# A new table of order and engine choices for an RWKV attention and Fourier-mixing kernel

## The chip, the cores and the metric

The kernel runs on one core of a Trainium2 chip. The metric is the device time of one execution in microseconds (us). A core has five engines with queues of their own, each in program order: TensorE (PE; its weight loads are listed as PEld), VectorE (DVE), ScalarE (ACT), GpSimd (POOL) and SyncE (SP), which here only issues transfers. ScalarE and GpSimd issue some transfers too. Semaphores order the engines among each other.

## The reference

Four batches, eight heads, 768 time steps, head size 48. First a linear attention with decay, then over its output x a two-dimensional Fourier transform of which the real part is added, a normalisation, and a two-layer network (384 to 1536 to 384) with a residual:

```python
for t in range(S):
    cur = np.einsum('bhd,bhe->bhde', u[None] * kt, vt)
    y[:, :, t] = np.einsum('bhd,bhde->bhe', rt, state + cur)
    state = w[None, :, :, None] * state + np.einsum('bhd,bhe->bhde', kt, vt)
...
X = np.fft.fft(np.fft.fft(x, axis=1), axis=2)
u = x + np.real(X)
un = (u - mu) / np.sqrt(var + 1e-06)
return u + np.maximum(un @ w_ch1, 0.0) @ w_ch2
```

## The kernel before

The time steps are cut into 24 chunks of 128 (six to a batch). For each chunk i: k, r and v are loaded (on SP). VectorE multiplies k and r by tables of decay powers into the bf16 tile KR (line 373, both operands in SBUF; the first two chunks in two halves, line 364, partly on GpSimd). KR is transposed to KRT, by TensorE and a copy (lines 393 to 398) for chunks 0 to 11, by a transposing DMA on SP (line 384) for 12 to 23. VectorE makes PR, the product of the k half and the r half of KRT (line 409, both operands in SBUF). TensorE makes the scores A (line 419) into two PSUM banks, one for the even heads and one for the odd ones; each is masked into MA either by a copy AC on ScalarE (line 426) and a select on GpSimd (line 428), or by VectorE straight out of PSUM (line 431). A bonus term de (line 482) is copied to DE (ScalarE, line 492) and multiplied with V into TT (GpSimd, line 493). The masked scores times V and the carried state make y (line 504). X is y plus TT: on VectorE as an addition (line 512), or, with TT added by an identity matmul `xt` (line 507) on TensorE, as a copy on ScalarE (line 514). The state S is carried on from chunk to chunk.

When the chunks of a batch are there, VectorE folds X into HH and XF (lines 527 and 533 for batch 0, chunk by chunk; 551, 558 and 566 for the others: all with both operands in SBUF). TensorE does the transform over time (fp, line 598), the result is evacuated to TT2 (ScalarE, line 606, or VectorE, line 607), reversed into TR (617), and TensorE transforms over the model dimension (mp, line 637). UF is x plus the result (VectorE, line 649, or ScalarE, line 652, behind an identity matmul `xr`), UB a bf16 version (lines 656 to 661), `st` and `MV` the statistics (666, 668). UB is transposed to UNT, by TensorE and a copy (676 to 680) for batch 0, by DMA for the others. A half batch (384 steps) is one unit hf of the network: 12 groups hp of three matmuls (line 713) with a Relu into HT on ScalarE (718) or VectorE (719), then for three row blocks j four groups mo of three matmuls each (line 733), the evacuation osb on VectorE (line 740) and the store (line 744 from GpSimd, 745 from SP).

Each of these steps is an entry in a list of operations with a number and, for some, several alternatives of engine. The table ORDER (line 97 on) gives the sequence in which the entries are emitted: `1123` is operation 1123 with its first alternative, `1124.1` the same with the second. `emit` plays it in that order: it hands each new tile the buffer of its ring that comes free first in the table, so the table decides the order in each engine's queue, the engine, and the buffers and PSUM banks. The operations numbered 0 to 149 are dummy matmuls over zeros (line 259, `idle`), of which a table takes as many as it likes.

```python
for k, (n, a) in enumerate(order):
    o = self.ops[n]
    for t in o["new"]:
        ends = held[t.ring]
        m = min(range(len(ends)), key=ends.__getitem__)
        ends[m] = last[t]
        t.value = self.rings[t.ring][m] if t.view is None else t.view(self.rings[t.ring][m])
    fn = o["alts"][a][2]
    if fn is not None:
        fn()
```

Of the kernel before, what the change touches and what calls it, by code (L numbers as in the profile page):

```python
# [97 lines left out]
170 152 158 173 159 160 166 193 162 150 163 161 171 168.1 174 151 175 153 0 1 2 182 205 155 164 165 154 183 186 187  # L98
172 202 203 178 185 167.1 169 156 184 199 200 299 3 4 5 6 7 8 302 303 300.1 190 9 304 305.1 188 10 307 191 189 192 196
274.1 275.1 310 195 206 208 209 325 11 12 329 327 328 330.1 331 13 14 15 332 198 214 333 16 339 179 340 277 350 279 17  # L100
18 352 278.1 280 282 201 276.1 207 326 335.1 287 157 353 311 281 334 197 289 336.1 285 181.1 211 212 354 375 223 355
308.1 290 21 22 283 356 286 19 20 377 180 291 204 379 378.1 380 23 24 25 382 381 288.1 309.1 385.1 306 215 400 292 284
194 26 27 293 301 312 213 220 294 295 314 376.1 28 402 315 313.1 342 317 210 337 383 341 343 403 404 405 224 338 357
358 316 386.1 29 407 464 364 365 389 408.1 409.1 217 218 351.2 362 318.1 319 320.1 344 296 345 410 177 468 366 226 384
390 363 391 466 467.1 367 469 30 31 471 392 406 412 387 360 423 33 388.1 32 425 426 427 221 443 216 361 445 446 347
447 413 401.1 368 176 297 346 359 369 298 411 35 428 34 430 370 448 450 431 348 433 227 485 321 322 323 393.1 394 371
372 395.1 219 424.2 487 415 324 414 374 416.1 488 271 396 273.1 417 418.1 489 373 397 37 490 419 36 813 806 807 349
222 1057 434 474 472 435 436.1 429 399 475 1055 814 815 799 800 816 792 437 438 229 230 451.1 452.1 420 422 232 421
398 449 491 506 432 801 233 802 444 453 793 794 795 796 797 817 818 798 819 803 804 808 809 810 470 527 439 440 805
# [693 lines left out]
```

## Time and profile before

| | |
|---|---|
| device time, median of 3 runs | 190.88 us (189.22 to 191.32) |
| the profiled execution | 190.09 us, of which its span is 188.2 us |
| mean granted TensorE clock | 0.989 of full speed |
| busy in the span: PE | 163.6 us (87%), 1592 matmuls |
| DVE | 150.1 us (80%), 350 instructions |
| ACT | 98.7 us (52%), 239 instructions |
| POOL | 84.2 us (45%), 124 instructions |

The span reaches from the first to the last instruction that the profile shows. A busy time is the time in which an engine ran at least one instruction. "Idle before" in a row is how long the engine stood still ahead of those instructions, with what released it. The granted clock is given as a share of full speed, 2.4 GHz.

### The profile page before, as it was taken

The numbers are of one execution on the slowest core, as the hardware profiler recorded it, in microseconds if no ns is written. First come the engines' busy times: TensorE is split into PE (matmuls) and PEld (weight loads), VectorE is DVE, ScalarE is ACT, GpSimd is POOL, SyncE is SP. The second block draws the span as 40 slices with busy tenths as digits, with TensorE's granted clock in tenths as the row PEclk, the third lists the DMA queues.
The fourth block names the chain that finished last, engine by engine and source line by source line (L and its number), as shares of the span: only waits on it lengthen the run. The fifth ranks groups of instructions, "written<-read, shape, count | busy, mean of one in ns | idle before, by whom it ended". The sixth has DMA issues, their size and how long they took to land.

```text
span 188.2 us, 4286 instructions
## 1 busy us (share of the span) xinstructions
PE 163.6 (87%) x1592; PEld 110.9 (59%) x1595; DVE 150.1 (80%) x350; ACT 98.7 (52%) x239; POOL 84.2 (45%) x124
## 2 busy tenths in 40 slices
PE   7987785947894996889899999899999999999990
PEld 1444463736772774566576677666677667666650
DVE  3479999997699999989989979998795868474240
ACT  3887566835872896654376765643384312311300
POOL 6748378491592453244761236576303411002131
PEclk9999999987999999999999999999999999999999
DMA  6999998999982996899999989891100361003222
GB/s 122 207 218 206 181 207 224 179 250 213 184 149 45 191 178 119 142 178 177 227 230 213 180 176 212 207 210 55 45 0 0 88 166 42 0 3 135 74 84 84
DMA packets 98341, 27.30 MB, mean 145 GB/s; under 512 B 95281, under 2 KB 96818, under 8 KB 98322
## 3 DMA queue, kind: packets, MB, share of 16 engines
q1 hardware_dynamic: 95808, 21.15, 58.1%
q0 software_dynamic: 2512, 5.90, 12.8%
q8 instruction: 12, 0.20, 0.4%
q14 instruction: 7, 0.06, 0.1%
q10 hardware_dynamic: 2, 0.00, 0.0%
HBM read 19.77 MB, written 4.72 MB: 130 GB/s over the span
## 4 chain that ended last, share of the span: by engine, by line
PE 44%; DVE 24%; issue 12%; DMA 10%; ACT 5%; POOL 2%; POOLq 0%; DVEq 0%; ACTq 0%
PE bank L713 17%; PE bank L733 12%; DMA KRT<-KR 8%; PE bank L598 4%; DVE PR L409 3%; DVE KR L373 3%; DVE X L512 2%; PE bank L637 2%; PE bank L259 2%; DMA UNT<-UB 2%; DVE MA L431 2%; POOL out_dram L744 2%; ACT AC L426 1%; PE bank L419 1%; DVE XF L533 1%
## 5 line engine op out<-in xcount | busy, mean ns | idle before, releaser
L713 PE MATMUL bank<-UNT,W 128*128 128x384 bf16 x288 | 54.2, 327 | 3.3 <-DVE X L512 2.4
L733 PE MATMUL bank<-W,HT 128*128 128x384 bf16 x288 | 52.7, 326 | 0.0
L718 ACT ACTIVATE HT<-bank 128x384 bf16<-128x384 f32 x67 | 30.1, 493 | 26.9 <-PE bank L713 25.6
L713 PEld LDWEIGHTS <-W 128*128 128x128 bf16 x288 | 30.8, 114 | 15.2 <-issue 3.5
L428 POOL TENSOR_SCALAR_AFFINE_SELECT MA<-AC 128x512 bf16<-128x512 bf16 x39 | 30.2, 780 | 17.7 <-ACT AC L426 17.4
L733 PEld LDWEIGHTS <-HT 128*128 128x128 bf16 x288 | 27.2, 98 | 16.4
L493 POOL TENSOR_TENSOR TT<-V,DE 128x384 bf16<-128x384 bf16 x24 | 21.6, 900 | 21.8 <-ACT DE L492 15.6
L426 ACT CAST AC<-bank 128x512 bf16<-128x512 f32 x39 | 22.3, 594 | 7.3 <-PE bank L419 5.8
L373 DVE TENSOR_TENSOR KR<-kr,wtab 128x768 bf16<-128x768 f32 x22 | 25.0, 1142 | 1.0 <-DMA kr<-in_r_dram 0.9
L744 POOL DMA_DIRECT2D out_dram<-osb x18 | 10.1, 561 | 33.6 <-DVE osb L740 31.4
L740 DVE SCALAR_TENSOR_TENSOR osb<-bank,rstd,UF 128x384 f32<-128x384 f32 x24 | 14.6, 611 | 11.2 <-PE bank L733 11.0
L719 DVE TENSOR_SCALAR HT<-bank 128x384 bf16<-128x384 f32 x29 | 15.2, 548 | 2.5 <-PE bank L713 2.5
L598 PE MATMUL bank<-te_t,XF 128*128 128x193 bf16 x108 | 13.7, 258 | 3.9 <-DVE XF L533 2.5
L259 PE MATMUL bank<-zero 128*128 128x512 bf16 x35 | 13.1, 468 | 2.7 <-DVE wuc L282 1.4
L409 DVE TENSOR_TENSOR PR<-KRT 128x512 bf16<-128x512 bf16 x24 | 14.5, 612 | 1.1 <-DMA KRT<-KR 0.5
L598 PEld LDWEIGHTS <-XF 128*128 128x128 bf16 x120 | 11.2, 105 | 6.1 <-DVE XF L533 2.7
L649 DVE SCALAR_TENSOR_TENSOR UF<-bank,X 128x384 f32<-128x384 f32 x22 | 11.5, 550 | 2.6 <-PE bank L637 2.4
L462 ACT CAST S<-bank 64x192 bf16<-64x192 f32 x30 | 9.4, 313 | 7.3 <-PE bank L450 4.0
L666 DVE BATCH_NORM_STATS2 st<-UF 128x6 f32<-128x384 f32 x24 | 13.0, 545 | 0.0
L419 PE MATMUL bank<-KRT 64*128 64x128 bf16 x192 | 9.8, 225 | 3.5 <-DMA KRT<-KR 2.3
L512 DVE TENSOR_TENSOR X<-bank,TT 128x384 bf16<-128x384 f32 x21 | 11.5, 546 | 1.6 <-PE bank L504 0.9
L419 PEld LDWEIGHTS <-KRT 64*128 64x128 bf16 x192 | 5.9, 97 | 11.2 <-issue 4.7
(95 smaller groups left out, 231.8 us busy)
## 6 DMA issues: line engine op xcount, KB each, us to landing
kr<-in_k_dram SPq DMA_DIRECT2D x24, 192.0 KB, 3.8
kr<-in_r_dram SPq DMA_DIRECT2D x24, 192.0 KB, 4.3
vt<-in_v_dram SPq DMA_DIRECT2D x24, 192.0 KB, 4.4
out_dram<-osb POOLq DMA_DIRECT2D x18, 192.0 KB, 2.3
W<-in_moe_w_ch_dram POOLq DMA_DIRECT2D x3, 384.0 KB, 5.0
W<-in_moe_w_ch_dram POOLq DMA_DIRECT2D x2, 576.0 KB, 7.5
out_dram<-osb SPq DMA_DIRECT2D x6, 192.0 KB, 1.9
te_t<-te_c SPq DMA_DIRECT2D x1, 579.0 KB, 5.4
```

The costliest lines, as they stand in the source:

```text
L259: op("idle", [("PE", "idle", lambda: nc.tensor.matmul(z(), lhsT=zero[:, 0:128], rhs=zero, start=True, stop=True))], r=["zero"], new=[z])
L373: one(("KR", i), "DVE", "KR", lambda: nc.vector.tensor_tensor(out=KR().rearrange("t s p (a d) -> t (s p) a d", a=2)[:, :, :, 0:D], in0=kr( ...
L409: one(("PR", i), "DVE", "PR", lambda: nc.vector.tensor_tensor(out=PR(), in0=KRT()[:, 0], in1=QTall(), op=AluOp.mult), r=kts, new=[PR], use ...
L419: nc.tensor.matmul(A_ps[a]()[:, p, :], lhsT=KRT()[rows, 0, p, :], rhs=QT(p, rows), start=(p == 0), stop=(p == NP - 1), skip_group_check=True)
L426: op(("AC", i, a), [("ACT", "AC", lambda: nc.scalar.copy(AC(), A_ps[a]())), ("NONE", "", None)], r=[("A", i)], w=[("AC", i, a)], new=[AC], ...
L428: op(("MA", i, a), [("POOL", "MA", lambda: nc.gpsimd.affine_select(out=MA[a](), in_=AC(), pattern=[[0, NP], [1, 128]], base=0, channel_mul ...
L493: one(("TT", i), "POOL", "TT", lambda: nc.gpsimd.tensor_tensor(out=TT(), in0=V(), in1=DE().unsqueeze(2).to_broadcast([128, H, D]), op=AluO ...
L512: op(("X", i), [("DVE", "X", lambda: nc.vector.tensor_tensor(out=X()[:, q, :], in0=yd()[:, 0:DM], in1=TT().rearrange("p h d -> p (h d)"), ...
L598: nc.tensor.matmul(fp()[:, par, :], lhsT=lhsT[:, g * CH:g * CH + 128], rhs=rhs, start=(nb == 0 and par == 0), stop=(nb == last and par == ...
L713: nc.tensor.matmul(hp(), lhsT=W1[:, dt, ft // 4 * 512 + ft % 4:(ft // 4 + 1) * 512:4], rhs=UNT()[:, :, dt, :], start=(dt == 0), stop=(dt = ...
L718: op(("HT", hf, ft), [("ACT", "HT", lambda: nc.scalar.activation(out=HT()[:, ft, :], in_=hp(), func=Act.Relu, scale=-1.0)), ("DVE", "HT", ...
L733: nc.tensor.matmul(mo(), lhsT=HT()[:, ft, j * 128:(j + 1) * 128], rhs=W2[:, ft, :], start=(ft == 0), stop=(ft == 11))
```

## The change

Only the table ORDER is replaced. It is described as a newly searched order of the same operations, played in order of time with the lock between VectorE and GpSimd and banks in program order. No operation is added or taken away but for dummy matmuls (38 before, 43 now); the alternatives change for some: masks MA on VectorE 9 to 17 (on GpSimd 39 to 31, with as many AC copies on ScalarE), X on ScalarE 3 to 10 (VectorE 21 to 14; as many identity matmuls `xt`), TT2 on VectorE 2 to 8, HT on VectorE 29 to 25, UF on ScalarE 2 to 5, UB on GpSimd 8 to 10 (VectorE 5 to 4), V on VectorE 6 to 7 and GpSimd 9 to 7, KRT copies on VectorE 7 to 10, S on VectorE 5 to 6, `tn` from VectorE to ScalarE, stores on SP 6 to 12 (GpSimd 18 to 12), the k and r loads of chunk 0 from SP to ScalarE's queue, and a few memsets at the start. The new table is one line longer, so its kernel's line numbers are higher by one (line 373 is 374 there).

```diff
 ORDER = """
-170 152 158 173 159 160 166 193 162 150 163 161 171 168.1 174 151 175 153 0 1 2 182 205 155 164 165 154 183 186 187
...
+181 205 150 151 154 157 156 202 155 164 152 158 165 172 153 166 179.1 159 162 208 160 209 170 199.1 200.1 176 177 206
...
```

**The first place: the last XF of batch 0.** In the rows a name is the tile that is written, then those that are read; the digit behind the name is the buffer. VectorE before, from the last part of batch 0's HH and XF on:

```order
L533 TENSOR_TENSOR XF0_100<-HH0_99 128x196
L409 TENSOR_TENSOR PR0_123<-KRT3_122 128x512
L533 TENSOR_TENSOR XF0_100<-HH0_99 128x196
L431 TENSOR_TENSOR MA0_130<-bank5_66,mtri_70 128x512
L527 TENSOR_TENSOR HH0_99<-X0_142 128x192
L533 TENSOR_TENSOR XF0_100<-HH0_99 128x196
L533 TENSOR_TENSOR XF0_100<-HH0_99 128x2x98 x2
L409 TENSOR_TENSOR PR2_125<-KRT2_121 128x512
L409 TENSOR_TENSOR PR3_126<-KRT1_120 128x512
L373 TENSOR_TENSOR KR4_94<-kr5_107,wtab1_78 128x16x48
L409 TENSOR_TENSOR PR1_124<-KRT0_119 128x512
L373 TENSOR_TENSOR KR2_92<-kr4_106,wtab2_79 128x16x48
```

GpSimd's queue at that place before, between the two loads of W1:

```order
L428 AFFINE_SELECT MA4_134<-AC0_127 128x512
L761 DMA W1_88<-in_moe_w_ch1_dram 128x3x768
L428 AFFINE_SELECT MA3_133<-AC1_128 128x512
L493 TENSOR_TENSOR TT0_139<-V2_116,DE1_137 128x384
L428 AFFINE_SELECT MA2_132<-AC2_129 128x512
L761 DMA W1_88<-in_moe_w_ch1_dram 128x3x768
L428 AFFINE_SELECT MA5_135<-AC0_127 128x512
```

VectorE now:

```order
L513 TENSOR_TENSOR X0_142<-bank1_62,TT2_141 128x384
L528 TENSOR_TENSOR HH0_99<-X0_142 128x192 x2
L534 TENSOR_TENSOR XF0_100<-HH0_99 128x196
L534 TENSOR_TENSOR XF0_100<-HH0_99 128x2x98
L528 TENSOR_TENSOR HH0_99<-X0_142 128x192
L410 TENSOR_TENSOR PR3_126<-KRT0_119 128x512
L528 TENSOR_TENSOR HH0_99<-X0_142 128x192
L380 CAST V4_118<-vt2_110 128x384
L534 TENSOR_TENSOR XF0_100<-HH0_99 128x196
L534 TENSOR_TENSOR XF0_100<-HH0_99 128x2x98
L513 TENSOR_TENSOR X1_143<-bank2_63,TT0_139 128x384
```

GpSimd now:

```order
L494 TENSOR_TENSOR TT0_139<-V0_114,DE0_136 128x384
L429 AFFINE_SELECT MA4_134<-AC1_128 128x512
L429 AFFINE_SELECT MA1_131<-AC0_127 128x512
L762 DMA W1_88<-in_moe_w_ch1_dram 128x3x768
L381 CAST V1_115<-vt4_112 128x384
L762 DMA W1_88<-in_moe_w_ch1_dram 128x3x768
L662 TENSOR_SCALAR UB0_179<-UF0_148,sm0_163 128x384
L381 CAST V3_117<-vt3_111 128x384
```

On VectorE the PR of chunk 6 and a mask stood among the last XF, and two PR and a KR followed; now the last XF follow a KR, a mask and an X, with one PR and one V between them. On GpSimd MA, TT, MA stood between the two loads of W1; now two masks stand ahead of them and a V between.

**The second place: KR of chunks 12 and 11, ahead of the network's first matmuls.** VectorE before; the first KR here is chunk 12's, the second chunk 13's:

```order
L409 TENSOR_TENSOR PR0_123<-KRT3_122 128x512
L512 TENSOR_TENSOR X1_143<-bank2_63,TT2_141 128x384
L649 SCALAR_TENSOR_TENSOR UF0_148,sm0_163<-bank6_67,X0_142 128x2x192
L373 TENSOR_TENSOR KR1_91<-kr1_103,wtab0_77 128x16x48
L512 TENSOR_TENSOR X1_143<-bank5_66,TT1_140 128x384
L719 TENSOR_SCALAR HT0_184<-bank4_65 128x384
L719 TENSOR_SCALAR HT0_184<-bank1_62 128x384
L373 TENSOR_TENSOR KR0_90<-kr0_102,wtab1_78 128x16x48
L409 TENSOR_TENSOR PR2_125<-KRT2_121 128x512
```

GpSimd before (the TT are those of chunks 8, 9 and 10):

```order
L493 TENSOR_TENSOR TT1_140<-V3_117,DE2_138 128x384
L661 TENSOR_SCALAR UB1_180<-UF0_148,sm0_163 128x384
L493 TENSOR_TENSOR TT0_139<-V4_118,DE1_137 128x384
L493 TENSOR_TENSOR TT2_141<-V0_114,DE0_136 128x384
L428 AFFINE_SELECT MA0_130<-AC0_127 128x512
L380 CAST V2_116<-vt0_108 128x384
L428 AFFINE_SELECT MA5_135<-AC2_129 128x512
L428 AFFINE_SELECT MA2_132<-AC0_127 128x512
```

VectorE now; the KR are those of chunks 9, 12 and 11:

```order
L374 TENSOR_TENSOR KR4_94<-kr4_106,wtab0_77 128x16x48
L618 COPY TR0_147<-TT20_145 97x768 x2
L374 TENSOR_TENSOR KR2_92<-kr2_104,wtab0_77 128x16x48
L399 COPY KRT2_121<-bank4_65 128x512
L410 TENSOR_TENSOR PR2_125<-KRT2_121 128x512
L650 SCALAR_TENSOR_TENSOR UF0_148,sm0_163<-bank7_68,X0_142 128x2x192
L667 BN_STATS st0_181<-UF0_148 128x6
L680 COPY UNT0_152<-bank1_62 128x384
L374 TENSOR_TENSOR KR1_91<-kr0_102,wtab2_79 128x16x48
L432 TENSOR_TENSOR MA3_133<-bank5_66,mtri_70 128x512
L680 COPY UNT1_153<-bank1_62 128x384
L680 COPY UNT1_153<-bank5_66 128x384
```

GpSimd now (the TT are those of chunks 9, 7, 10 and 8):

```order
L429 AFFINE_SELECT MA2_132<-AC1_128 128x512
L662 TENSOR_SCALAR UB1_180<-UF1_149,sm1_164 128x384 x2
L494 TENSOR_TENSOR TT1_140<-V1_115,DE2_138 128x384
L494 TENSOR_TENSOR TT2_141<-V2_116,DE0_136 128x384
L494 TENSOR_TENSOR TT0_139<-V3_117,DE1_137 128x384
L429 AFFINE_SELECT MA0_130<-AC2_129 128x512
L429 AFFINE_SELECT MA5_135<-AC2_129 128x512
L494 TENSOR_TENSOR TT2_141<-V4_118,DE2_138 128x384
L429 AFFINE_SELECT MA5_135<-AC0_127 128x512
L765 DMA W2_89<-in_moe_w_ch2_dram 128x1536
```

On VectorE the KR of chunk 12 has moved ahead of all UF and UNT of batch 0, and that of chunk 11, which stood further up (the second KR of the first place), now stands among the UNT; five masks of chunks 9 to 11 are on VectorE here, of which the rows show the first (L432, behind the KR of chunk 11) and the others follow within nine rows. On GpSimd three TT follow each other behind two UB, and then come two masks, a TT and a mask.

## Rows read from the trace of the kernel before

**Rows 1.** Windows, each: length, busy PE, PEld, DVE, ACT, POOL, PEclk, DMA share, GB/s.

```profile
5.80:41.00 35.20, 27.00 (x336) 16.90 (x338) 31.51 (x69) 24.66 (x58) 23.77 (x29) 1.00 1.06 210
41.00:44.00 3.00, 3.00 (x22) 2.52 (x22) 2.95 (x5) 1.80 (x3) 1.79 (x2) 0.50 1.15 209
...
60.00:140.00 80.00, 74.82 (x786) 52.52 (x784) 73.94 (x169) 49.33 (x125) 37.20 (x53) 1.00 0.84 164
140.00:183.20 43.20, 43.12 (x287) 28.46 (x284) 25.25 (x66) 11.34 (x26) 8.20 (x14) 1.00 0.21 63
```

**Rows 2.** Chain that ended last, in order of time: start us, us, what.

```profile
153.93 8.29 PE bank L713 x51
```

**Rows 3.** Timelines, 37 to 41 us: start us, us, instruction, [idle before].

```profile
37.07 0.26 DVE L533 TENSOR_TENSOR XF<-HH 128x196 bf16<-128x196 bf16 x1
...
38.13 2.64 DVE L533 TENSOR_TENSOR XF<-HH 128x196 bf16<-128x196 bf16 x3
...
38.56 0.65 POOL L428 TENSOR_SCALAR_AFFINE_SELECT MA<-AC 128x512 bf16<-128x512 bf16 x1
39.17 0.83 POOL L493 TENSOR_TENSOR TT<-V,DE 128x384 bf16<-128x384 bf16 x1
39.96 0.66 POOL L428 TENSOR_SCALAR_AFFINE_SELECT MA<-AC 128x512 bf16<-128x512 bf16 x1
...
40.83 0.34 PE L598 MATMUL bank<-te_t,XF 128*128 128x193 bf16 x1 [2.50 <-DVE XF L533]
```

**Rows 4.** Timelines of VectorE, GpSimd and TensorE, 54 to 61 us.

```profile
55.08 3.61 DVE L373 TENSOR_TENSOR KR<-kr,wtab 128x768 bf16<-128x768 f32 x1
...
60.01 0.94 DVE L373 TENSOR_TENSOR KR<-kr,wtab 128x768 bf16<-128x768 f32 x1
60.87 0.41 DVE L409 TENSOR_TENSOR PR<-KRT 128x512 bf16<-128x512 bf16 x1
...
54.64 1.60 POOL L493 TENSOR_TENSOR TT<-V,DE 128x384 bf16<-128x384 bf16 x2
56.21 0.62 POOL L428 TENSOR_SCALAR_AFFINE_SELECT MA<-AC 128x512 bf16<-128x512 bf16 x1
56.79 0.49 POOL L380 CAST V<-vt 128x384 bf16<-128x384 f32 x1
57.25 0.62 POOL L428 TENSOR_SCALAR_AFFINE_SELECT MA<-AC 128x512 bf16<-128x512 bf16 x1
...
59.21 0.48 PE L713 MATMUL bank<-UNT,W 128*128 128x384 bf16 x2 [2.36 <-DVE X L512]
```

**Rows 5.** Groups by line, VectorE, 0 to 60 us: busy us, mean ns.

```profile
L373 DVE TENSOR_TENSOR KR<-kr,wtab 128x768 bf16<-128x768 f32 x11 | 14.1, 1288 | 0.1
L409 DVE TENSOR_TENSOR PR<-KRT 128x512 bf16<-128x512 bf16 x11 | 7.2, 658 | 0.6 <-ACT KRT L397 0.5
L533 DVE TENSOR_TENSOR XF<-HH 128x196 bf16<-128x196 bf16 x12 | 5.4, 462 | 0.1
```

**Rows 6.** Groups by line, the whole span.

```profile
L428 POOL TENSOR_SCALAR_AFFINE_SELECT MA<-AC 128x512 bf16<-128x512 bf16 x39 | 30.2, 780 | 17.7 <-ACT AC L426 17.4
...
L512 DVE TENSOR_TENSOR X<-bank,TT 128x384 bf16<-128x384 f32 x21 | 11.5, 546 | 1.6 <-PE bank L504 0.9 <-POOL MA L428 0.5
...
L431 DVE TENSOR_TENSOR MA<-bank,mtri 128x512 bf16<-128x512 f32 x9 | 6.1, 681 | 0.0
...
L607 DVE CAST TT<-bank 97x386 bf16<-97x386 f32 x2 | 1.2, 603 | 2.2 <-PE bank L598 2.2
```

**Rows 7.** DMA issues: transfers, KB each, median us from issue to landing.

```profile
kr<-in_k_dram SPq DMA_DIRECT2D x24, 192.0 KB, 3.8
...
W<-in_moe_w_ch_dram POOLq DMA_DIRECT2D x2, 576.0 KB, 7.5
...
te_t<-te_c SPq DMA_DIRECT2D x1, 579.0 KB, 5.4
hid_t<-hid_c SPq DMA_DIRECT2D x1, 288.0 KB, 6.4
```

97 rows, old and new, of the table ORDER are left out of this document.

## The prediction, made before the changed kernel ran

> **What bounds the kernel now.** I read the windows first. From 60 to 140 us TensorE is busy 74.8 of 80 us and from 140 to 183.2 us it is busy 43.1 of 43.2; in the first stretch, 5.8 to 41 us, it is busy only 27.0 of 35.2 while VectorE is busy 31.5 [rows 1]. So VectorE sets the pace until batch 0 has gone through the Fourier step, TensorE sets it afterwards, and the last 5.0 us of the 188.2 us span (183.2 to the end) are the last evacuation and its store. Between 60 and 140 both are close to full: VectorE is busy 73.9 of 80.
>
> Next I looked for the places where TensorE stood still after 30 us, in the timelines. There are two large ones, and both begin on VectorE.
>
> The first: three XF instructions of batch 0 took 2.64 us together, though one alone takes 0.26. Three GpSimd instructions ran through just that time, back to back from 38.56 to 40.62, and the first transform matmul behind XF then had waited 2.50 us [rows 3]. Right after it the granted clock is 0.50 from 41 to 44 us, the lower of the two levels, 1.2 GHz [rows 1]: TensorE had been idle and came back slow.
>
> The second: one KR product took 3.61 us, where the next took 0.94. GpSimd ran five instructions from 54.64 to 57.87 without a gap, and KR ended 0.8 us later, about one KR. Behind it on VectorE stood an X evacuation, and the matmuls of the first layer waited 2.36 us for it [rows 4].
>
> So a VectorE instruction that reads two SBUF operands does not make progress beside GpSimd here; it can lose several turns in a row. Over the first 60 us the loss is: KR 11 x (1.288 - 0.94) = 3.8 us, PR 11 x (0.658 - 0.41) = 2.7, XF 12 x (0.462 - 0.26) = 2.4, together 8.9 [rows 5], against the undisturbed 0.26 [rows 3] and 0.94 and 0.41 [rows 4]. Of these, 1.9 and 2.7 are the two places above; 4.3 are spread.
>
> **The change part by part.** The operations are the same; the table moves nearly all of them and picks other engines for some.
>
> First, the engines. VectorE gets 8 more masks (MA) at 0.68 = +5.4 us and 6 more TT2 evacuations at 0.60 = +3.6; 7 X go to ScalarE at 0.55 = -3.8; of the remaining small ones (HT, UF, UB, tn off, KRT, S, V on) nine leave and five come, four net at about 0.55 = -2.2 [rows 6]. Net +3.0 us in the whole span. How much of it lies ahead of the first MLP matmuls? By adding the same durations along the two tables I find that up to the last UNT of batch 0 the new one holds about 2.3 us less VectorE work than the old. I take neither as a term: +3.0 lies mostly after 60 us beside TensorE, -2.3 is the cushion for it. If that cover failed, each would cost or give its own size, so the bounds are -2.3 and +3.0.
>
> GpSimd loses 8 masks at 0.78 = -6.2 us [rows 6], and six stores and two V go elsewhere. ScalarE loses eight AC copies and gains seven X; it is busy 52% of the span (page 1), so I price that at nothing. Its idle time hides it; if it had none, X on it costs about what it saves on VectorE.
>
> TensorE gets work for this: an X on ScalarE needs a 384-column identity matmul (seven more), and so do three UF on ScalarE. A 384-column matmul costs 8.29 / 51 = 0.163 us in a run [rows 2], ten make **+1.6 us**. TensorE is full in the second half, so I count it all. Five more dummy matmuls stand ahead of the last XF of batch 0, where TensorE has 35.2 - 27.0 = 8.2 us free [rows 1]: nothing. Without that cover they would cost 5 x 0.163 x 512 / 384 = 1.1 us, by their 512 columns.
>
> Second, the order at place one. In the old table GpSimd's queue holds MA, TT, MA between two W1 loads here; they were ready while VectorE came to the last three XF. In the new one VectorE does four XF in one run earlier, GpSimd's last mask stands ahead of the last four, and what follows on GpSimd is one mask, a W1 load, which only issues, a V and the other W1 load. So the 2.64 us should become 0.6: **-2.0 us**. If the XF follow without a gap, TensorE is not idle for 2.5 us and the half clock from 41 to 44, 3.0 us of work done at half speed, should not come: **-1.5 us**. Below: nothing, when another gap takes its place; the most is both.
>
> Third, place two. KR of chunk 12 stood ahead of the first MLP matmuls amid two TT, two MA and a V on GpSimd. In the new table it stands much earlier, behind TR of batch 0, and five masks of chunks 9 to 11 that GpSimd would have had are on VectorE here, reading PSUM. The wait of TensorE goes: **-2.4 us**.
>
> Fourth, the rest of the loss. GpSimd has about 13% less work ahead of batch 0's last XF (again by adding durations along the tables). 13% of the remaining 4.3 us is **-0.6 us**. Bounds: nothing, and half, 2.1.
>
> Fifth, what is late next. KR(12) moved forward needs its data earlier. Loads run at 210 GB/s in this stretch with the DMA engines' share at its top, 1.06 [rows 1], so I take that as all they give: 36 loads of 192 KB and the two tables (867 KB with hid) [rows 7] are about 7.8 MB, 37 us at that rate; the two W1 loads, 576 KB each [rows 7], may come before it, another 5.5. With the 3.8 us that the first one takes to land, r(12) is there between 41 and 46 us. KR(12) on VectorE is due near 43: XF ended at about 40.8 [rows 3], 2.0 less makes 38.8, and behind it come an X (0.55), a TT2 (0.60), two PR (0.41 each), S and KR(9) (about 0.55, and 0.94) and two TR (about 0.4 each). Wait: 0 to 3 us, with KRT(9), PR(9) and UF(0,2) queued behind. I take **+1.5 us**, the middle, since whether the W1 loads come before it decides.
>
> SP's queue now has 12 stores among loads and transposes, before 6. Each waits for its osb, and what is behind it waits too. The osb stand well ahead of the K-transposes behind them in the table, so I price this at nothing; one osb that is late by one MLP group of three matmuls costs 0.5 us.
>
> The sum: 188.2 + 1.6 - 2.0 - 1.5 - 2.4 - 0.6 + 1.5 = 184.8 us span. The profiled execution took 190.09, 1.9 us more than its span, which gives 186.7. The median of the runs is 190.88, 0.8 above the profiled one; I leave this in the range. So **186.7 us**, 2.2% under the median.
>
> **The rivals.**
>
> A. As above: 186.7, from 185.2 (KR(12) finds its data: -1.5) to 188.2 (the clock still falls or KR(12) waits 3 us, either +1.5).
>
> B. The lock loss falls everywhere, not only in two places: the spread loss halves (2.1 for 0.6) and of the 5.2 us that TensorE is idle between 60 and 140 us half goes: 184.8 - 1.5 - 2.6 + 1.9 = 182.6. For: 8 of the masks have left GpSimd. Against: many short VectorE instructions still stand next to GpSimd's in the table.
>
> C. No change: the first 50 us are as much bound by loads as by VectorE. What VectorE gains it spends waiting for KR(12), KR(11) and the ones behind, +4.5 in place of +1.5: 184.8 + 3.0 + 1.9 = 189.7. (4.5 is what places one and two give beside the clock: 2.0 + 2.4.) For: the rate of 210 GB/s does not change. Against: KR waited for next to nothing in the first 60 us before, 0.1 us [rows 5].
>
> D. Slower, by a new starved instruction. KR(11) now stands among a run of nine GpSimd instructions (three UB, TT(9), then TT(7), TT(10), MA, MA, TT(8)); behind it on VectorE wait UNT copies of batch 0, and so every MLP matmul. From KR(11) on, three TT at 0.80 and two MA at 0.62 and the one in progress, 0.80, make 4.4 us [rows 4]; with TensorE idle that long the clock falls again, 1.5. With another stall of the same kind at KR(14) or KR(13), in the same run of masks, of 2.7: 184.8 + 8.6 + 1.9 = 195.3; with KR(11) alone 192.6. It is slower than the profiled execution when KR(11) is held for more than 190.1 - 186.7 = 3.4 us, or 1.9 with the clock falling. For: the rows show just that with a run of five. Against: TT waits for its DE from ScalarE, which breaks runs.
>
> The Trainium skill, SBUF — State Buffer, "Who interferes with whom", says that the instruction that issues first holds the shared pair for its whole length and the other blocks. Read as one turn, this would limit the loss of a KR to the rest of one GpSimd instruction. The trace differs: KR lost 2.7 us over four or five of them [rows 4]. By the rule D would cost at most 0.8 and the time would be 187.5; I go by the row.
>
> **How the numbers follow.** A 0.43, B 0.16, C 0.20, D 0.21. The likeliest is A. About 1% (1.9 us) is what a measurement of this kernel can tell from no change: under 189.0 is faster, over 192.8 slower. B and nearly all of A are faster: 0.55. C and a little of A and D are the same: 0.25. Most of D is slower: 0.20. The range leaves out half of D and some of B: 182 to 193.5; A's own is 185.2 to 188.2.
>
> **What would show it.** The three last XF of batch 0 take under 1 us together, and the granted clock is 1.0 in the 5 us behind them. No KR in the first 60 us is over 2 us. TensorE's first MLP matmuls run without a gap of over 1 us, some 3 us earlier. From 140 us on TensorE is full, as before. I am wrong if a KR or PR of 3 us shows near the first MLP matmuls (D), or if KR waits for a load there (C).

## The result, and the profile after

The changed kernel took 182.14 us (median of 4 runs), the kernel before 190.62 beside it: a ratio of 0.954, with an interval of 0.944 to 0.963. It is faster by 4.6%, where 2.2% was forecast; the time lies at the lower end of the range. The profiled execution took 182.16 us, its span is 180.5, 7.7 less than before. Single executions of one kernel differ by some per cent (the kernel before: mostly near 190.7 us, in the later comparisons some near 188; one of the four here took 186.33), and a ratio compares the faster executions of both sides, so some gains below are given by the medians and by the ratio.

A number in brackets behind a name is that of a chunk, or of a batch for XF, TR and UF; numbers behind it count parts of it: KR(12) is chunk 12's, XF(1) batch 1's.

The windows of the changed kernel (length, busy PE, PEld, DVE, ACT, POOL, PEclk, DMA share, GB/s):

```profile
0.00:5.80 5.80, 3.04 (x6) 1.07 (x7) 2.24 (x17) 2.61 (x4) 3.82 (x13) 1.00 0.77 148
5.80:41.00 35.20, 29.89 (x369) 19.08 (x368) 30.18 (x72) 25.27 (x62) 17.65 (x24) 1.00 1.11 211
41.00:44.00 3.00, 3.00 (x37) 2.00 (x36) 3.00 (x6) 2.56 (x7) 1.02 (x3) 1.00 1.07 144
41.00:60.00 19.00, 18.64 (x234) 13.45 (x233) 17.04 (x38) 15.76 (x45) 10.54 (x16) 1.00 1.09 173
60.00:140.00 80.00, 77.60 (x790) 54.68 (x788) 71.28 (x173) 44.01 (x110) 35.71 (x52) 1.00 0.81 159
140.00:175.50 35.50, 35.50 (x222) 22.67 (x220) 19.75 (x51) 8.98 (x21) 4.47 (x8) 1.00 0.23 67
```

Two windows of the kernel before, for the stretches that [rows 1] does not have:

```profile
0.00:5.80 5.80, 4.40 (x9) 1.35 (x10) 2.72 (x17) 2.36 (x4) 3.67 (x12) 1.00 0.70 135
...
41.00:60.00 19.00, 14.29 (x183) 11.69 (x182) 16.07 (x31) 10.98 (x30) 10.76 (x16) 0.91 0.83 149
```

TensorE's idle is length less busy. It goes from 1.40 to 2.76 at the head (the dummies start later), from 8.20 to 5.31 up to 41 us, from 4.71 to 0.36 up to 60, and from 5.18 to 2.40 up to 140; behind 140 there is none in either. That is 8.7 us less in all. TensorE's busy time rises by 1.2, from 163.6 to 164.9, so the two give 7.5 of the 7.7; the rest lies behind the last window. The granted clock from 41 to 44 us is 1.00, where it was 0.50 [rows 1].

The two places, in the timelines of VectorE and GpSimd (start us, us, instruction, [idle before]):

```profile
37.23 0.56 DVE L534 TENSOR_TENSOR XF<-HH 128x196 bf16<-128x196 bf16 x2
...
38.65 0.55 DVE L534 TENSOR_TENSOR XF<-HH 128x196 bf16<-128x196 bf16 x2
...
43.15 0.95 DVE L374 TENSOR_TENSOR KR<-kr,wtab 128x768 bf16<-128x768 f32 x1
...
46.90 0.95 DVE L374 TENSOR_TENSOR KR<-kr,wtab 128x768 bf16<-128x768 f32 x1
...
47.59 2.52 POOL L494 TENSOR_TENSOR TT<-V,DE 128x384 bf16<-128x384 bf16 x3 [0.68 <-ACT DE L493]
```

The last four XF take 0.56 and 0.55 us by twos, where three took 2.64 [rows 3]. KR(12), at 43.15, takes 0.95 and waits for no load. KR(11), at 46.90, takes 0.95 as well: it starts as GpSimd goes idle for 0.68 us, waiting for a DE, and has run 0.7 us when TT starts.

VectorE's groups from 0 to 60 us (busy us, mean ns | idle before):

```profile
L374 DVE TENSOR_TENSOR KR<-kr,wtab 128x768 bf16<-128x768 f32 x13 | 13.4, 1034 | 4.7 <-DMA kr<-in_r_dram 4.7
...
L410 DVE TENSOR_TENSOR PR<-KRT 128x512 bf16<-128x512 bf16 x12 | 6.2, 513 | 1.1 <-ACT KRT L398 0.9
...
L534 DVE TENSOR_TENSOR XF<-HH 128x196 bf16<-128x196 bf16 x12 | 2.7, 256 | 0.1
```

Reckoned as in the prediction, the loss to GpSimd is 13 x (1.034 - 0.94) + 12 x (0.513 - 0.41) = 2.5 us, XF loses nothing, where it was 8.9 [rows 5]. The 4.7 us that a KR waits for a load is at the head of the kernel.

What TensorE still waits for from 41 to 140 us is little; these are its rows in the timeline with an idle time behind 48 us:

```profile
66.34 1.51 PE L599 MATMUL bank<-te_t,XF 128*128 128x193 bf16 x10 [0.24 <-DVE XF L567]
71.09 0.33 PE L451 MATMUL bank<-V,KR 128*128 128x96 bf16 x4 [0.83 <-POOL V L381]
77.73 1.14 PE L734 MATMUL bank<-W,HT 128*128 128x384 bf16 x6 [0.15 <-DVE osb L741]
107.00 0.65 PE L714 MATMUL bank<-UNT,W 128*128 128x384 bf16 x3 [0.78 <-DVE X L513]
```

The kernel before has more and longer ones in the same view; some of them:

```profile
46.64 0.33 PE L488 MATMUL bank<-S,KRT 128*128 128x96 bf16 x4 [1.20 <-ACT DE L492]
...
73.66 0.26 PE L598 MATMUL bank<-te_t,XF 128*128 128x193 bf16 x1 [1.06 <-DVE XF L566]
...
80.23 0.40 PE L419 MATMUL bank<-KRT 64*128 64x128 bf16 x8 [0.69 <-DMA KRT<-KR]
...
92.46 0.65 PE L713 MATMUL bank<-UNT,W 128*128 128x384 bf16 x3 [0.85 <-DVE HT L719]
```

So the forecast's two places went as it said, and beside them a dozen smaller waits went, most of them on DE, XF, KRT and HT, which it had left as they were.

### The profile page after: what moved, and what is told of

Same layout as the page of the kernel before. It is cut to its first block, busy times and chain, and to the rows that moved or that the text cites. A ratio compares the mean times of both kernels' runs of the same rounds, so it can differ in the third digit from the quotient of the medians.

```text
span 180.5 us, 4284 instructions
## 1 busy us (share of the span) xinstructions
PE 164.9 (91%) x1610; PEld 110.9 (61%) x1610; DVE 141.2 (78%) x349; ACT 96.6 (54%) x238; POOL 72.7 (40%) x111
## 4 chain that ended last, share of the span: by engine, by line
PE 32%; issue 27%; DVE 12%; ACT 9%; DMA 8%; POOL 5%; SPq 5%; POOLq 0%; DVEq 0%; ACTq 0%
PE bank L734 8%; PE bank L714 8%; DMA kr<-in_r_dram 5%; SPq L343 4%; DMA KRT<-KR 3%; PE bank L420 2%; ACT AC L427 2%; PE bank L638 2%; DVE KR L374 2%; PE bank L599 2%; POOL out_dram L745 2%; PE bank L505 2%; ACT KRT L398 1%; PE bank L489 1%; PE bank L451 1%
## 5 line engine op out<-in xcount | busy, mean ns | idle before, releaser
L714 PE MATMUL bank<-UNT,W 128*128 128x384 bf16 x288 | 52.6, 327 | 0.8 <-DVE X L513 0.8
L719 ACT ACTIVATE HT<-bank 128x384 bf16<-128x384 f32 x71 | 31.8, 500 | 23.1 <-PE bank L714 22.9
L429 POOL TENSOR_SCALAR_AFFINE_SELECT MA<-AC 128x512 bf16<-128x512 bf16 x31 | 21.5, 700 | 23.9 <-ACT AC L427 21.5
L374 DVE TENSOR_TENSOR KR<-kr,wtab 128x768 bf16<-128x768 f32 x22 | 22.8, 1041 | 6.7 <-DMA kr<-in_r_dram 6.7
L745 POOL DMA_DIRECT2D out_dram<-osb x12 | 6.7, 560 | 42.1 <-DVE osb L741 42.1
L427 ACT CAST AC<-bank 128x512 bf16<-128x512 f32 x31 | 17.5, 592 | 6.6 <-PE bank L420 5.4
L720 DVE TENSOR_SCALAR HT<-bank 128x384 bf16<-128x384 f32 x25 | 13.2, 550 | 9.7 <-PE bank L714 9.7
L410 DVE TENSOR_TENSOR PR<-KRT 128x512 bf16<-128x512 bf16 x24 | 11.9, 496 | 1.1 <-ACT KRT L398 0.9
L432 DVE TENSOR_TENSOR MA<-bank,mtri 128x512 bf16<-128x512 f32 x17 | 11.5, 684 | 0.8 <-PE bank L420 0.6
L394 PE MATMUL bank<-ident,KR 128*128 128x128 bf16 x96 | 8.4, 219 | 2.3 <-DVE KR L374 1.4
```

Source lines behind the costliest of these rows:

```text
L374: one(("KR", i), "DVE", "KR", lambda: nc.vector.tensor_tensor(out=KR().rearrange("t s p (a d) -> t (s p) a d", a=2)[:, :, :, 0:D], in0=kr( ...
L427: op(("AC", i, a), [("ACT", "AC", lambda: nc.scalar.copy(AC(), A_ps[a]())), ("NONE", "", None)], r=[("A", i)], w=[("AC", i, a)], new=[AC], ...
L429: op(("MA", i, a), [("POOL", "MA", lambda: nc.gpsimd.affine_select(out=MA[a](), in_=AC(), pattern=[[0, NP], [1, 128]], base=0, channel_mul ...
L714: nc.tensor.matmul(hp(), lhsT=W1[:, dt, ft // 4 * 512 + ft % 4:(ft // 4 + 1) * 512:4], rhs=UNT()[:, :, dt, :], start=(dt == 0), stop=(dt = ...
L719: op(("HT", hf, ft), [("ACT", "HT", lambda: nc.scalar.activation(out=HT()[:, ft, :], in_=hp(), func=Act.Relu, scale=-1.0)), ("DVE", "HT", ...
L720: ("DVE", "HT", lambda: nc.vector.tensor_scalar(out=HT()[:, ft, :], in0=hp(), scalar1=-1.0, scalar2=0.0, op0=AluOp.mult, op1=AluOp.max))],
```

## The experiments

### Where in the order the gain lies

The table is put together of a first part of one order and, behind it, whatever is left in the other's order, each operation with the engine of the table that it comes from:

```python
head = first[:k]
held = {n for n, _ in head}
table = head + [(n, a) for n, a in then if n not in held]
```

The changed kernel's first 460, then before's rest:

> The first 460 operations of the new table (to about 53 us of its run), then what is left in the old table's order. Theory 1 (the gain comes from the first stretch, where VectorE instructions with two SBUF operands no longer starve beside GpSimd, so the network's first matmuls start earlier and without a gap): most of the 8.5 us, 183.5 to 186. Theory 2 (the choice of engines, masks and X, over the whole program): it has about half of these choices, 185 to 188. Theory 3 (the gain comes from the part after 60 us, where TensorE's idle time fell from 5.2 to 2.4 us between 60 and 140): 187 to 190.

Measured: 187.44 us, ratio 0.985 (0.980 to 0.989): 3.1 us less. That is outside the range of theory 1 and inside those of 2 and 3.

Before's first 460, then the new rest:

> The reverse: the first 460 operations of the old table (to about 60 us of its run), then what is left in the new table's order. Theory 1: little gain, 187.5 to 190. Theory 2: 185 to 188. Theory 3: most of the gain, 184 to 186.5. If this run and e1 together gain more or less than the whole change, the two halves depend on each other.

Measured: 193.14 us, ratio 1.015 (1.008 to 1.023): 2.6 us more, outside all three ranges. The two parts gain 3.1 - 2.6 = 0.5 us when each is taken alone and 8.5 together, so they depend on each other.

The new order up to 600:

> The first 600 operations in the new order (up to some 70 us, through the fold of batch 1), the others in the old one; the run with 460 stopped at some 50 us, before that fold, and gave 187.4. Theory: what is gained by the last XF(1) stands (6.9 us in the changed kernel), and the rest is work at TensorE's pace in either order: 183.7, at most 1.3 more, as the run with 460 operations gave back behind its XF(1), so up to 185.0. Rival, the stretch between 50 and 70 us is no better in the new order and only the whole belongs together: 187 or more.

Measured: 187.40 us (185.33 to 189.71), against 190.70 of the kernel before.

The new order up to 840:

> The first 840 operations in the new order (up to some 99 us, the last XF(2)), the others in the old one. XF(2) ends 10.2 us earlier in the changed kernel than before, its end 7.7 earlier. Theory, TensorE's pace sets the end from here in either order: 182.1 to 183.4. Rival, the old tail doesn't fit (other work is left over for it) and gives back 2 us and more: 184 or more.

Measured: 185.00 us, ratio 0.984 (0.977 to 0.990). The gain is 5.7 us by the medians and 3.0 by the ratio.

The first 50 us of the new order are worth 3.1 of the 8.5 us, the first 70 us no more that can be told (3.3), the first 99 us 3.0 by the ratio and 5.7 by the medians, and the tail behind them the rest. With 600 operations the last XF(1) is 6.2 us earlier than before, and the end only 3.3. TensorE then waits for what batch 2 and the network have not made ready; rows of its timeline in that run:

```profile
79.67 0.40 PE L420 MATMUL bank<-KRT 64*128 64x128 bf16 x8 [1.09 <-DMA KRT<-KR]
87.63 0.65 PE L714 MATMUL bank<-UNT,W 128*128 128x384 bf16 x3 [0.86 <-DVE HT L720]
105.34 0.40 PE L420 MATMUL bank<-KRT 64*128 64x128 bf16 x8 [1.25 <-DMA KRT<-KR]
```

The theory for both later cuts, that TensorE's pace keeps whatever is gained by XF(1) or XF(2), fell: a milestone that is early is worth only what the work behind it is ready to use.

### Engines and order apart

Each operation keeps its place, and takes the engine that the other table gives it:

```python
table = [(n, dict(other)[n]) for n, a in order]
```

The old order with the new engines (but for MA(3,0), MA(9,1) and MA(11,1)):

> The old order with the new table's engines, for all operations where the buffers allow it (three masks stay as they were). Theory 1: the order is what keeps GpSimd away from KR, PR and XF, so the stalls stay in another place, 187.5 to 191; VectorE's loss to GpSimd stays above 12 us of the old 17. Theory 2: with 8 masks and two V fewer on GpSimd the loss falls below 10 us, and the time is 183 to 186.

Measured: 208.71 us, ratio 1.096 (1.091 to 1.101).

The new order with the old engines (but for MA(4,0) and MA(20,0)):

> The new order with the old engines (two masks stay as they are in the new one). Theory 1: the places of the order that the text speaks of stay free, most of the gain stays, 183 to 186. Theory 2: GpSimd is as loaded as before and the gain is gone, 188 to 191. An order searched for one choice of engines may stall at places of its own with another; the VectorE loss and the place of TensorE's gaps tell that from theory 2.

Measured: 203.33 us, ratio 1.060 (1.053 to 1.066).

Neither half gains anything; mixed, they lose 13 to 18 us, outside all ranges. The engine shares alone are not the cause, and a smaller loss to GpSimd by itself is not either. VectorE's groups from 0 to 60 us, in the old order with the new engines:

```profile
L374 DVE TENSOR_TENSOR KR<-kr,wtab 128x768 bf16<-128x768 f32 x10 | 10.4, 1038 | 0.7 <-ACT wtab L316 0.7
L410 DVE TENSOR_TENSOR PR<-KRT 128x512 bf16<-128x512 bf16 x11 | 6.2, 579 | 0.8 <-ACT KRT L398 0.8
...
L534 DVE TENSOR_TENSOR XF<-HH 128x196 bf16<-128x196 bf16 x12 | 3.2, 278 | 0.1
```

Reckoned as above, its loss is 3.1 us, near the 2.5 of the changed kernel and far from the 8.9 before. Yet TensorE is idle for 11.8 us between 60 and 140, where it was 5.2 before and is 2.4 in the changed kernel.

### The two places alone

The kernel before gets two tiny copies on GpSimd that wait for VectorE, so that GpSimd can't run beside the instructions that lost their turns:

```diff
+    op("hold0", [("POOL", "hold", lambda: nc.gpsimd.tensor_copy(hold[:, 0:4], bat[0]["XF"]()[:, 1, 1, 0:4]))],
+       use=[bat[0]["XF"]])
+    op("hold1", [("POOL", "hold", lambda: nc.gpsimd.tensor_copy(hold[:, 4:8], kr12()[:, 0, 0, 0:4]))], use=[kr12])
...
-398 449 491 506 432 801
+398 449 491 506 1395 432 801
...
-558 482 523 483 522
+558 482 523 483 1396 522
```

> The kernel before with two tiny GpSimd copies (4 columns each) that make GpSimd wait: one just ahead of MA(6,1), which reads the output of XF(0,4,0), and one just ahead of TT(10), which reads KR(12). So VectorE cannot lose the shared port in the two places on which the forecast's gain rests (2.64 us for three XF at 38.13, 3.61 us for KR(12) at 55.08). Theory of the forecast: 2.0 + 1.5 (clock) + 2.4 us come off, so 190.6 falls to 184.7, and the granted clock at 41 to 44 us is 1.0. Rival 1, the stall only moves to the next VectorE instructions (PR and KR behind XF, X behind KR), since GpSimd does the same work later: 188.5 to 190.6. Rival 2, VectorE is slack there and nothing is gained: 190 to 191, with short XF and KR(12) in the trace.

Measured: 187.56 us, ratio 0.989 (0.979 to 0.998): 3.1 us less by the medians, about half of the 5.9, and 2.2 by the ratio. Its timeline, and two of its windows:

```profile
38.16 0.73 DVE L534 TENSOR_TENSOR XF<-HH 128x196 bf16<-128x196 bf16 x3
...
43.55 2.24 DVE L618 COPY TR<-TT 97x768 bf16<-97x768 bf16 x1
...
53.50 1.21 DVE L374 TENSOR_TENSOR KR<-kr,wtab 128x768 bf16<-128x768 f32 x1
...
43.17 0.33 PE L489 MATMUL bank<-S,KRT 128*128 128x96 bf16 x4 [1.20 <-ACT DE L493]
45.84 1.27 PE L638 MATMUL bank<-hid_t,TR 97*128 97x192 bf16 x12 [1.47 <-DVE TR L618]
...
44.00:47.00 3.00, 1.53 (x18) 1.15 (x16) 3.00 (x5) 0.84 (x3) 1.56 (x3) 1.00 1.20 219
47.00:50.00 3.00, 2.96 (x41) 2.27 (x39) 2.76 (x10) 2.62 (x9) 0.83 (x2) 0.59 1.11 211
```

XF falls from 2.64 us to 0.73 and KR(12) from 3.61 to 1.21, as wanted. But GpSimd's work now runs beside TR, which takes 2.24; TensorE waits for it, is busy 1.53 us of the three from 44 on, and the clock falls in the next three, to 0.59. Place one gave all that the forecast had for it at first: the matmul at 43.17 is 3.5 us earlier than before (46.64). At the first network matmul 1.0 us of it is left (52.03 for 53.01). Place two kept its gain: the wait of 2.36 us is gone, TensorE's first wait for XF(1) ends 3.6 us earlier than before (68.75 for 72.34), and the span is 3.3 shorter.

A third copy makes GpSimd wait for TR too (ahead of entry 454, MA(7,0)):

```diff
+    op("hold2", [("POOL", "hold", lambda: nc.gpsimd.tensor_copy(hold[0:97, 8:12], tr0()[0:97, 2, 0:4]))], use=[tr0])
```

> The run with two holds and a third one: GpSimd also waits ahead of MA(7,0) until TR(0,1) is done. With two holds the three XF ran in 0.73 us, but the two TR then took 2.24 us beside GpSimd at 43.55, TensorE waited 1.47 for them at 45.84 and ran at 0.59 of its clock from 47 to 50. Theory, the port is lost to the next VectorE copy whenever GpSimd has work behind, and the half clock comes with the gap: TR falls to some 0.7, and 1.5 to 2.7 us more come off, so 184.9 to 186.1. Rival, GpSimd's delay (1 to 2 us on MA(7,0), TT(7)) comes back as a wait for y(7) or V(8): 187 to 188.5.

Measured: 187.33 us, ratio 0.993 (0.987 to 0.998); no more than with two, and inside the rival's range. In the profiled execution (188.60 us) the two TR take 0.61 us, TensorE waits for ScalarE instead, and the clock is 0.50 from 50 to 53:

```profile
43.53 0.61 DVE L618 COPY TR<-TT 97x768 bf16<-97x768 bf16 x2
...
47.84 0.24 PE L483 MATMUL bank<-UW,PR 128*128 128x2 bf16 x4 [1.02 <-ACT UF L653]
49.35 0.33 PE L489 MATMUL bank<-S,KRT 128*128 128x96 bf16 x4 [1.02 <-ACT DE L493]
```

So at place one another wait came in for each that was taken away. Whether that is the old order's doing or that of the holds, which also make GpSimd's own work late, these runs do not tell apart. The two places alone are worth 3.1 us, as much as the new order's first 460 operations.

### The half clock alone

Thirteen matmuls with weights of zero fill TensorE's wait at place one in the kernel before:

```diff
+    for n in range(13):
+        op(("warm", n), [("PE", "warm", lambda: nc.tensor.matmul(
+            fp00().rearrange("p a m -> p (a m)"), lhsT=zero[:, 0:128], rhs=zero[:, 0:386], start=False, stop=False,
+            skip_group_check=True))], use=[fp00])
```

> The kernel before with thirteen matmuls with weights of zero (128x386, 0.161 us each at full clock, they add zeros) between fp(0,0,3) and fp(0,0,4), where TensorE waits 2.50 us for XF(0,4,0) and then runs at clock 0.50 from 41 to 44 us. They fill some 2.1 us of that wait and delay nothing that the trace shows ready. Theory of the forecast: the clock stays at 1.0 and its term of 1.5 us comes off alone, 190.6 to 189.1. Rival: TensorE has enough idle behind it to catch up without (3.7 us between 40 and 50), so 190.3 to 191.0 with the clock at 1.0; or the clock falls all the same.

Measured: 191.06 us median of ten, ratio 1.001 (0.996 to 1.006). In the profiled execution they ran for 2.29 us and the clock was 1.00 from 41 to 44 us:

```profile
38.19 2.29 PE L774 MATMUL bank<-zero 128*128 128x386 bf16 x13
...
41.00:44.00 3.00, 2.87 (x48) 2.49 (x47) 3.00 (x6) 2.14 (x5) 1.81 (x2) 1.00 1.06 163
```

In that execution (193.72 us) TensorE's wait for DE that ended at 46.64 in the kernel before ends 1.6 us earlier, at 45.07, as the term has it. At 50.92 a wait of 2.33 us for a UF from ScalarE ends, and then the clock falls after all:

```profile
53.00:56.00 3.00, 3.00 (x30) 2.62 (x28) 2.06 (x6) 1.05 (x5) 2.84 (x5) 0.50 1.07 198
```

It is one execution, and longer than the median. But two of the ten, with a mean clock of 0.999, took 189.06 and 189.40, which is what the term of 1.5 would give, and in the later comparisons the five executions of the kernel before with a mean clock of 0.998 or more took 187.62 to 188.83. So filling this one wait gains nothing in the median; that the half clock costs nothing does not follow.

### A stall put back into the new order

Four dummy masks on GpSimd (entries 1395 to 1398) behind MA(6,1):

```diff
+    for n in range(4):
+        op(("late", n), [("POOL", "late", lambda: nc.gpsimd.affine_select(
+            out=late, in_=zero, pattern=[[1, 512]], base=0, channel_multiplier=-1, compare_op=AluOp.is_gt, fill=0.0))])
...
-432 418.1
+432 1395 1396 1397 1398 418.1
```

> The changed kernel with four dummy affine_selects of 128x512 on GpSimd right behind MA(6,1), where the last XF instructions of batch 0 run on VectorE (36.5 to 39 us). They put back the kind of stall that the kernel before had at place one. If VectorE's path there sets the end: 2 to 2.5 us of stall come through in full, and up to 1.5 more by half clock if TensorE idles over 2 us, so 184.1 to 186.2. Rival, what follows has slack and takes it up: 182.1 to 183.0.

Measured: 184.93 us, against 182.14 without: 2.8 us more, inside what the path through VectorE predicts.

```profile
36.43 2.79 POOL L775 TENSOR_SCALAR_AFFINE_SELECT late<-zero 128x512 bf16<-128x512 bf16 x4
...
40.29 1.10 DVE L535 TENSOR_TENSOR XF<-HH 128x196 bf16<-128x196 bf16 x2
...
41.45 0.26 PE L600 MATMUL bank<-te_t,XF 128*128 128x193 bf16 x1 [2.23 <-DVE XF L535]
...
41.00:44.00 3.00, 2.55 (x26) 2.46 (x26) 2.72 (x7) 1.54 (x3) 1.00 (x2) 0.75 1.03 162
44.00:47.00 3.00, 3.00 (x27) 1.89 (x25) 2.34 (x4) 1.86 (x4) 0.00 (x0) 0.68 1.15 201
```

The last two XF start 1.6 us later (40.29 for 38.65) and take 1.10 for 0.55. The clock is 0.75 and 0.68 in the six microseconds from 41 on: 3 x 0.25 + 3 x 0.32 = 1.7 us of work lost. The first network matmuls are 3.5 us late, 0.5 of it is made up by 131 us. So in the new order a stall of this kind with its half clock costs 3.5 us at the network's start, what the forecast had for place one in the old (2.0 + 1.5), and 2.8 at the end. The masks also add 2.8 us to GpSimd's queue; that the cost came through XF is read from TensorE's wait for it.

### More work for TensorE

Each xt matmul is issued twice, the second time with weights of zero:

```diff
-        op(("xt", i), [("NONE", "", None), ("PE", "xt", lambda: nc.tensor.matmul(
-            yd()[:, 0:DM], lhsT=ident, rhs=TT().rearrange("p h d -> p (h d)"), start=False, stop=False,
+        op(("xt", i), [("NONE", "", None), ("PE", "xt", lambda: [nc.tensor.matmul(
+            yd()[:, 0:DM], lhsT=m, rhs=TT().rearrange("p h d -> p (h d)"), start=False, stop=False,
...
+            skip_group_check=True) for m in (ident, zero[:, 0:128])])],
```

> The changed kernel with each of its ten xt matmuls followed by a second one of the same size with weights of zero (it adds zeros): 10 x 0.163 = 1.63 us more on TensorE, which is what the forecast's first term was. Theory of the forecast (TensorE is the bound wherever it is full, so its work goes on the end at full price): 182.1 rises to 183.7. Rival, most of these stand where TensorE waits for others anyway (10.8 us of idle in the changed kernel): 182.1 to 182.8.

Measured: 182.37 us, 0.2 more, which is nothing that can be told: the rival. The last XF(1) comes 1.3 us later than in the changed kernel's profile, and the last XF(3) at the same time. Most of the 1.3 is not the added matmuls: this execution ran at a clock of 0.66 from 10 to 15 us, and so did that of the new order up to 600, with the same table so far and single xt, where the last XF(1) comes 0.7 later. Between XF(1) and XF(3) stands V(13), for which GpSimd waits on a load; in the changed kernel, and then with the doubled matmuls:

```profile
70.54 0.50 POOL L381 CAST V<-vt 128x384 bf16<-128x384 f32 x1 [5.35 <-DMA vt<-in_v_dram]
```

```profile
69.07 0.50 POOL L381 CAST V<-vt 128x384 bf16<-128x384 f32 x1 [2.61 <-DMA vt<-in_v_dram]
```

TensorE's wait of 0.83 us for V(13) is gone in the second, where the load also landed 1.5 us earlier. So what was late by a microsecond ahead of this load was not late behind it. Five of the ten xt run before 34 us, where TensorE still has idle time, and only one behind 60 in the changed kernel.

### The loads that are left

Entry 240, v(13), goes ahead of 244, k(15), and 263, r(21), ahead of 267, v(22):

```diff
-595 597 566 577 244 1075
+595 597 566 577 240 244 1075
...
-938 717 948 262 267 1190.1
+938 717 948 262 263 267 1190.1
```

> The changed kernel with two loads earlier on SP's queue: v(13) ahead of k(15) (GpSimd waits 5.35 us for it at 65 to 70 us, then TensorE 0.83 for V(13)), and r(21) ahead of v(22). Theory, TensorE is near full behind 40 us, so only its own idle there can be won: at most 0.83 + 0.78 us, so 180.5 to 182.1. Rival, loads that go ahead push others back (k(15), k(22)) and the wait moves: 182.1 to 183.5.

Measured: 184.83 us (183.31 to 185.22), 2.7 slower than the changed kernel; the rival, and more than it said. TensorE no longer waits for V(13), but for what now comes later:

```profile
78.12 0.40 PE L420 MATMUL bank<-KRT 64*128 64x128 bf16 x8 [0.75 <-DMA KRT<-KR]
...
92.84 3.12 PE L714 MATMUL bank<-UNT,W 128*128 128x384 bf16 x18 [0.87 <-DMA UNT<-UB]
```

### Two KR of batch 2 moved back into the fold of batch 1

In the changed kernel KR(14) and KR(13) stand ahead of that fold. Here they and what hangs on them were to follow the last XF(1). In fact they stand behind two of its four instructions; 556 and 555, the other two, come after them:

```diff
-1123 852 473 853 593 832 1079
+1123 852 473 853 832 1079
...
-552 553 554 557 556
+552 553 554 557 593 575 595 597 577 598 556
```

> The changed kernel with KR(13) and KR(14), and what hangs on them there (KRT(14), A(14), KRT(13), AC(14,1)), put behind the last XF(1), where the kernel before has KR(14). Theory (the new order gains behind 60 us since the transposes of batch 2 are ready before TensorE wants them, where the kernel before waits 0.28 + 0.69 + 0.48 us for KRT at 79 to 85): the last XF(1) ends up to 1.9 us earlier (two KR of 0.95 less ahead of it), but TensorE then waits for KRT by 1 to 2.5 us, and the end is 183.0 to 184.6. Rival, it doesn't matter which comes first, since TensorE has MLP matmuls for the meantime: 181.5 to 182.7.

Measured: 190.15 us, ratio to the kernel before 1.008 (1.004 to 1.012). The whole gain is gone, three times the most that the theory expected.

```profile
58.81 0.56 DVE L552 TENSOR_TENSOR EO<-X 128x768 bf16<-128x768 bf16 x1 [1.97 <-ACT X L515]
...
64.20 1.03 DVE L567 TENSOR_TENSOR XF<-HH 128x588 bf16<-128x588 bf16 x2
65.16 1.81 DVE L374 TENSOR_TENSOR KR<-kr,wtab 128x768 bf16<-128x768 f32 x2
66.89 0.84 DVE L567 TENSOR_TENSOR XF<-HH 128x588 bf16<-128x588 bf16 x2
...
66.24 2.73 SPq L385 DMA_TRANSPOSE KRT<-KR  x2
...
70.11 0.61 PE L420 MATMUL bank<-KRT 64*128 64x128 bf16 x8 [7.55 <-DMA KRT<-KR]
...
66.00:72.00 6.00, 1.89 (x13) 1.01 (x14) 2.16 (x5) 1.14 (x3) 0.53 (x1) 0.50 1.00 185
```

A(14) stands in TensorE's queue ahead of the Fourier matmuls of batch 1 and of network matmuls, and now waits for its KRT, whose transpose is issued at 66.24 and lets it start at 70.11. XF(1) is complete at 67.7, 1.1 us later than in the changed kernel, and its matmuls stand still behind A(14); the clock is 0.50 from 66 to 72. So the run prices one matmul group that stands in TensorE's queue ahead of its operands. It is not the old arrangement: in the kernel before A(14) stands behind nearly all of these Fourier matmuls. The first row tells something else: without the two KR, VectorE waits 1.97 us ahead of the fold for an X from ScalarE (0.35 in the changed kernel), and the fold starts no earlier (58.81 for 58.90). In the new order these two KR, 1.9 us of VectorE, stand in time that was free anyway.

## Why the prediction was wrong

The direction and the places were right, the size was not: the span fell by 7.7 us and the forecast's sum had 3.4.

**Place one and its clock (-2.0, -1.5), place two (-2.4).** Each went in the trace as said. For place one the price holds in the new order: a stall put back there cost 2.8 us. In the old order the two stalls, taken away alone, gave 3.1 of the 5.9 (2.2 by the ratio). What went missing is place one's: its 3.5 us were there at 43 us, and then TR, or UF and DE with a third hold, made TensorE wait, and the half clock came 6 to 9 us later. The step did give the lower bound, "another gap takes its place", but took the upper. The price of place two in the new order was not measured.

**The spread loss (-0.6).** It was mis-sized: the whole loss of KR, PR and XF fell from 8.9 to 2.5. Less the 1.9 and 2.7 of the two places, the spread part fell from 4.3 to 2.5, by 1.8 and not 0.6. The measure for it, 13% less work on GpSimd, was too small: GpSimd was busy 17.65 us from 5.8 to 41 where it was 23.77, 26% less. How much of the fall is this and how much is which instructions stand beside each other is not shown. Nor does such a loss turn into time by itself: with the new engines in the old order the loss is 3.1 and the kernel takes 208.71 us.

**The identity matmuls (+1.6).** Mis-sized: "TensorE is full in the second half, so I count it all". Ten more xt on top cost 0.2 us. Nine of the ten run before 60 us and not in that half, and TensorE's waits behind them, one of them for a load at 71 us, take up what is late: its idle time from 60 to 140 us fell from 2.40 to 1.26 in that run. A misreading beside it: of the five added dummies only two stand ahead of the last XF of batch 0; three run behind it, at 41.6 and 49.0 us, where TensorE is nearly full. By the prediction's own price they are 3 x 0.22 = 0.7 us that the sum has at nothing; no run here takes them out.

**KR(12) waits for r(12) (+1.5).** It did not come: KR(12) starts at 43.15 behind TR without an idle time. The middle of 0 to 3 us was taken, and 0 was right.

**TensorE's other waits (nothing).** This is the step that failed most. Between 41 and 60 us 4.35 us of idle went, of which 2.36 are place two's; between 60 and 140 another 2.78. The 4.8 us that are not place two's are more than the 4.3 by which the sum fell short; the 1.5 of KR(12) come on top, and against both stand 1.4 us more idle time at the head and 1.1 us more busy time than the sum had. The sum kept these waits as they were without giving a reason; only rival B let half of those behind 60 us go. The cuts of the order show that they hang on the table's later part, order and engines together: with only the first 460 or 600 operations new, 5.3 of the 8.5 us are missing by the medians, and KRT and HT make TensorE wait again. That part alone, behind the old start, loses 2.6 us. Which of the later moves does most of it stays open; the run with two KR moved shows that a single such place can be worth 8 us, not that it is the one that the kernel before lacked.

**The rivals.** B, 182.6, came nearest: its signs, the loss halved everywhere and half of the idle from 60 to 140 us gone (5.18 to 2.40), are both in the trace. That the first is the cause of the second is not shown, and the old order with the new engines speaks against it: there the loss falls to 3.1 and the idle time rises to 11.8. C did not come: no KR between 10 and 60 us waits for a load. D did not come: KR(11) met GpSimd while it waited for DE, as the sentence against D said.

**The rule of the Trainium skill** (SBUF — State Buffer, "Who interferes with whom") that I set aside for the row of KR(12) would have put D at 0.8 at most. The page says it of VectorE's two-port modes; of an instruction with two SBUF inputs, such as KR, it says that it contends with GpSimd's reads. In the changed kernel the longest KR of the full size took 1.58 us, 0.64 over an undisturbed one, less than the one TT that started ahead of it (0.93 us, at 20.91). That is as the rule has it:

```profile
21.08 1.58 DVE L374 TENSOR_TENSOR KR<-kr,wtab 128x768 bf16<-128x768 f32 x1
```

So this row agrees with the rule and the 3.61 us of [rows 4] do not; they stay without an explanation of their own.

## What to carry to other kernels

A stall that is seen in a trace is priced by what waits next: taking away the two largest alone gave half of their price, what the first of them gave was mostly lost again within 9 us, and taking away a third gave nothing. When the whole order is made anew, look at all idle of the engine that bounds each stage, not only at its largest pieces, and ask for each whether the work or the order makes it. Work added to the engine that bounds a stage can be free when it falls into that engine's idle time or ahead of a later wait, so look where it stands before pricing it; and one instruction of an in-order queue that is ready late costs all that stands behind it.

## What the hardware showed unexpectedly

The half clock does not hang on one long wait. Behind the wait of 2.36 us ahead of 59.21 in the kernel before [rows 4] it did not come: the clock is 1.00 from 60 us on [rows 1]. It followed a single wait of 2.50 us in the kernel before, one of 2.23 in the run with the dummy masks, and two of 1.20 and 1.47 with work between them in the run with two holds (0.59 from 47 to 50). In the profiled executions of the kernel before and of its three variants with holds or a filled wait it came between 41 and 56 us, whichever wait there was taken away (0.50 from 41 to 44, 0.59 from 47 to 50, 0.50 from 50 to 53 and from 53 to 56). A copy of four columns that waits for VectorE's result is enough to keep GpSimd from running beside it: it brought KR(12) from 3.61 to 1.21 us, and took 0.2 to 0.3 us itself. Dummy masks beside XF also became slower themselves, four in 2.79 us, 0.70 each where a mask of that size takes 0.62 [rows 4].
